# An adaLN block on one core: the second gate moved from w2 to the finished tiles, its weights loaded late, and a new instruction order

## The chip, the cores and the metric

The kernel runs on one core of a Trainium2 chip. A core has five engines, each with its own instruction queue that is worked off in order: TensorE (PE, matrix products; PEld is its weight load), VectorE (DVE), ScalarE (ACT), GpSimd (POOL) and SyncE (SP, which here issues nearly all DMA transfers). They are held together by semaphores alone: an instruction that waits holds up everything behind it in its queue. The metric is the device time of one execution in microseconds (us); the profile's span runs from the first to the last instruction.

## The reference

x has 2048 rows of 512 numbers in bf16. A condition c gives six vectors: two shifts, two scales, two gates.

```python
mod = (_silu(c) @ w_mod).reshape(c.shape[0], 6, 1, -1)
sa, ca, ga, sb, cb, gb = (mod[:, 0].copy(), mod[:, 1].copy(), mod[:, 2].copy(), mod[:, 3].copy(), mod[:, 4].copy(), mod[:, 5].copy())
h = _layernorm(x, axis=-1) * (1 + ca) + sa
x = x + ga * _A_ref(h, A_wqkv, A_wo)
h = _layernorm(x, axis=-1) * (1 + cb) + sb
x = x + gb * _B_ref(h, B_w1, B_w3, B_w2)
```

`_A_ref` is attention with 32 heads of 16, in which a row looks at eight rows: itself and those 2, 4, ... 14 rows before it. `_B_ref` is `(silu(h @ w1) * (h @ w3)) @ w2` with 1792 hidden columns. gb is the second gate: it multiplies the columns of the feed-forward output before it is added to x.

## The kernel before

The rows are cut into 16 tiles T of 128. Everything stays in on-chip memory but v, which goes through a scratch tensor in DRAM so that the shifted rows can be gathered by DMA.

The program is written as a list of operations (`p.op`, `p.dma`, line 82 on), each with its engine and the values that it reads and writes. It is not emitted in the order of the text: the table `ORDER` (line 980) is a permutation of all operations, and each engine gets its own operations in that order. `SLOTS` (line 1028) says which buffer of its pool (PSUM bank, q, v, vsh, output buffer and so on) each value gets. Waits follow from both: for the values read, and for the earlier users of a buffer. The numbers beside each operation (its cost) are only notes for whoever made the order; they change nothing in the instructions.

The stages, as the text has them:

- **Constants and loads.** SP issues x, w_mod in pieces (`wm_s` for shifts and scales, `wm_g` for the gates; `wm_g[i]` lie in a region that the feed-forward stage later takes for its hidden tiles), wqkv, wo, w1, w3, w2 in four parts each.
- **Modulation.** Per output column a few matmuls with one moving column. `gate(i)` (line 522) makes gate i: 16 small matmuls from `wm_g[i]`, `gcol` copied by DVE (537), four matmuls that spread it over all partitions (541), and an ACT copy to `ga_bc` or `gb_bc` (547). ga is multiplied into wo (946), gb into w2 in four parts (952, values `w2_scaled`), both on DVE.
- **First layer norm, q, k, v** over the groups `LN1`: tiles 0-1, 2-3, then fours. `ln_stats` (549) takes mean and variance on DVE (555, 556), adds epsilon (DVE for tiles 0 and 1, POOL otherwise), raises to -1/2 on POOL (565), and normalizes on DVE (576; tile 0 has a form of its own, 571). It runs over pairs of tiles, for tiles 0 and 1 over each tile alone. `ln_T` (609) transposes on PE (636) or by DMA (617) and applies scale and shift, on ACT (644, 621) or, for the first half of the first group, on DVE (651). For the first group the projections run piece by piece, one input quarter at a time (`pieces`, 611, and `proj`, 665).
- **Attention**, in blocks of two tiles (the last of four): products of q with shifted k on DVE (742), sums over a head on PE (752), maximum, subtraction, sum, reciprocal and weights on DVE (764 to 797), exponential on ACT (782), a turn of the weights on PE (807) and its copy by ACT (811), products with the gathered v on DVE (827), sums on PE (855), a copy by ACT (861), a DMA transpose, the output projection (867) and the residual on DVE (871), which also sums x for the next norm.
- **Second layer norm** (`ln_sums`, 582): minus the mean on POOL (586), squares on ACT (590), then three steps on POOL (596 variance, 597 power, 599 bias), the normalized tiles on ACT (601); transposes and shift/scale as above.
- **Feed-forward** over the groups `FFN`: tiles 0-1, 2-3, 4-7, 8-11, 12-13, 14-15. Per group and hidden block fi of 128 columns (14 blocks): four matmuls with w1 (883), silu on ACT (889), four with w3, the product on DVE (892). Then per tile `ffn_w2` (899): 14 matmuls of 512 columns in two halves into one PSUM bank (921), for tiles 14 and 15 in two column halves (909), and `store`: DVE adds x (931) and SP stores.

PE, DVE and ACT work at several stages at once: the feed-forward of early groups stands between the attention of later tiles.

## Time and profile before

| | |
|---|---|
| times of three runs | 239.48, 238.94, 238.96 us (median 238.96) |
| profiled execution | span 237.7 us; 1.26 below the median of the runs |
| granted TensorE clock | 1.000 |
| loads through the main DMA queue | 38.56 MB |
| DMA transposes of normalized tiles, issue to landing | 3.7 us (median of 20) |
| loads of 512 KB parts of w1, w3, w2, issue to landing | 7.9 us (median of 6) |

In the views, a row of the timeline gives start and length in us, engine, line, operation, output and inputs by the program's names, how many instructions were merged, and in brackets the idle time before it with what ended it. `pall` is PSUM. A row of a group gives busy time, mean duration in ns, and idle time before. In the table by stage the columns are the stretch, its length, and the busy time (and number of instructions) of PE, PEld, DVE, ACT and POOL, then the clock, the DMA share and GB/s. Matmuls are pipelined: one of 512 columns shows as 379 ns, while a new one starts every 216.

### The profile page before, as it was taken

To read this page: it belongs to the slowest core of one execution; us is meant where nothing else is said; L and a number is where in the kernel's file an instruction comes from. 1 tells how busy PE (TensorE), PEld (TensorE's weight loads), DVE (VectorE), ACT (ScalarE), POOL (GpSimd) and SP (SyncE) were. 2 spreads that over 40 slices of the span, in tenths; PEclk is the share of its full clock that TensorE was granted. 3 is DMA by queue.
4 is the path that set the end of the run, shared out by engine and by line. 5 is a ranking of instruction groups with operands and counts; after the bars stand their busy time and mean duration, and the time that the engine had idled before them with its cause. 6 is when DMAs were issued, how large, how long until landed. Compare 5 with 4: busy or idle time off the path is not lost.

```text
span 237.7 us, 4535 instructions
## 1 busy us (share of the span) xinstructions
PE 229.7 (97%) x1781; PEld 136.2 (57%) x1806; DVE 179.4 (75%) x279; ACT 138.5 (58%) x267; POOL 29.2 (12%) x66
## 2 busy tenths in 40 slices
PE   7999999999999998999999999999999999999995
PEld 4776454445588674664444444444475457485774
DVE  5699999999999989999999999682654403434433
ACT  2289577999978744985865594837473405040300
POOL 4434100013002000240002520012010000000000
PEclk9999999999999999999999999999999999999999
DMA  6999999999999999897981693642203000000202
GB/s 216 372 337 322 158 237 299 208 269 283 353 200 270 243 249 199 173 260 177 247 234 47 182 234 72 154 132 46 67 19 91 3 0 0 6 19 0 70 0 88
DMA packets 46317, 38.85 MB, mean 163 GB/s; under 512 B 21704, under 2 KB 37080, under 8 KB 46296
## 3 DMA queue, kind: packets, MB, share of 16 engines
q1 hardware_dynamic: 46288, 38.56, 66.9%
q8 instruction: 14, 0.23, 0.4%
q14 instruction: 7, 0.06, 0.1%
q10 hardware_dynamic: 8, 0.00, 0.0%
HBM read 29.62 MB, written 4.21 MB: 142 GB/s over the span
## 4 chain that ended last, share of the span: by engine, by line
PE 74%; DMA 8%; DVE 8%; SPq 4%; ACT 3%; issue 2%; ACTq 0%; DVEq 0%
PE pall L883 38%; PE pall L921 18%; DMA sb_x<-in_A_x_dram 5%; PE pall L867 5%; SPq L124 4%; PE pall L691 4%; DMA sb_vsh<-v_scratch_dram 3%; PE pall L909 3%; PE pall L855 2%; PE pall L752 2%; PE pall L711 2%; DVE sb_vsh L827 2%; DVE sb_pq L742 2%; DVE sb_hh L892 1%; ACT sb_h L621 1%
## 5 line engine op out<-in xcount | busy, mean ns | idle before, releaser
L883 PE MATMUL pall<-sb_h,sb_w 128*128 128x256 bf16 (+1 forms) x664 | 101.9, 307 | 1.8 <-DVE sb_hh L892 0.9
L883 PEld LDWEIGHTS pall<-sb_h,sb_w 128*128 128x128 bf16 x672 | 64.8, 98 | 37.2 <-issue 2.8
L889 ACT ACTIVATE sb_sg<-pall 128x256 bf16<-128x256 f32 (+1 forms) x84 | 35.6, 453 | 54.1 <-PE pall L883 53.0
L892 DVE TENSOR_TENSOR sb_hh<-sb_sg,pall 128x256 bf16<-128x256 bf16 (+1 forms) x84 | 39.9, 505 | 34.8 <-PE pall L883 32.7
L921 PE MATMUL pall<-sb_w,sb_hh 128*128 128x512 bf16 x190 | 44.0, 379 | 0.3
L742 DVE TENSOR_TENSOR sb_pq<-sb_q,sb_kT 128x4096 bf16<-128x4096 bf16 x16 | 36.3, 2282 | 0.0
L921 PEld LDWEIGHTS pall<-sb_w,sb_hh 128*128 128x128 bf16 x196 | 19.0, 98 | 21.6 <-DVE sb_hh L892 0.4
L691 PE MATMUL pall<-sb_h,sb_wqkv 128*128 128x512 bf16 (+1 forms) x154 | 30.2, 335 | 0.5 <-issue 0.2
L827 DVE TENSOR_TENSOR sb_vsh<-sb_vsh,sb_al 128x4096 bf16<-128x4096 bf16 x12 | 27.3, 2287 | 2.1 <-DMA sb_vsh<-v_scratch_dram 2.1
L621 ACT ACTIVATE sb_h<-sb_h,sb_modc 128x512 bf16<-128x512 bf16 (+1 forms) x24 | 16.5, 743 | 10.1 <-DMA sb_h<-sb_xn 10.1
L691 PEld LDWEIGHTS pall<-sb_h,sb_wqkv 128*128 128x128 bf16 x160 | 14.7, 98 | 11.8 <-ACT sb_ac L861 0.4
L931 DVE TENSOR_TENSOR sb_o<-pall,sb_x 128x512 bf16<-128x512 f32 (+1 forms) x18 | 11.1, 625 | 10.5 <-PE pall L921 6.8
L711 PE MATMUL pall<-sb_wqkv,sb_h 128*128 128x512 bf16 x62 | 15.5, 379 | 0.2
L867 PE MATMUL pall<-sb_wo,sb_ot 128*128 128x512 bf16 x61 | 15.3, 379 | 0.3 <-issue 0.2
L586 POOL TENSOR_SCALAR sb_nm<-sb_sx 128x2 f32<-128x2 f32 x8 | 1.7, 218 | 105.2 <-DVE sb_x L871 105.1
L644 ACT ACTIVATE sb_h<-pall,sb_modc 128x256 bf16<-128x256 bf16 (+1 forms) x18 | 9.9, 612 | 7.5 <-DVE sb_modc L509 6.5
L861 ACT ACTIVATE sb_ac<-pall 128x512 bf16<-128x512 f32 x16 | 9.5, 595 | 7.2 <-PE pall L855 7.1
L601 ACT ACTIVATE sb_xn<-sb_x,sb_nb,sb_rs 128x512 bf16<-128x512 bf16 x16 | 12.4, 806 | 0.7 <-POOL sb_nb L599 0.6
L871 DVE SCALAR_TENSOR_TENSOR sb_x<-pall,sb_x 128x512 bf16<-128x512 f32 x16 | 10.9, 686 | 1.5 <-PE pall L867 1.3
L590 ACT ACTIVATE sb_xn<-sb_x,sb_nm 128x512 bf16<-128x512 bf16 x16 | 11.4, 714 | 0.7 <-POOL sb_nm L586 0.7
L721 ACT ACTIVATE sb_v<-pall 128x512 bf16<-128x512 f32 x16 | 9.5, 600 | 2.8 <-PE pall L711 2.8
L555 DVE BATCH_NORM_STATS2 sb_st<-sb_x 128x6 f32<-128x512 bf16 x16 | 10.6, 680 | 0.8 <-DMA sb_x<-in_A_x_dram 0.7
(87 smaller groups left out, 208.3 us busy)
## 6 DMA issues: line engine op xcount, KB each, us to landing
sb_vsh<-v_scratch_dram SPq DMA_DIRECT2D x48, 256.0 KB, 5.5
sb_vshx<-v_scratch_dram SPq DMA_DIRECT2D x16, 256.0 KB, 4.6
sb_w<-in_B_w_dram SPq DMA_DIRECT2D x6, 512.0 KB, 7.9
sb_w<-in_B_w_dram SPq DMA_DIRECT2D x6, 384.0 KB, 5.4
v_scratch_dram<-sb_v SPq DMA_DIRECT2D x16, 128.0 KB, 6.4
out_dram<-sb_o SPq DMA_DIRECT2D x14, 128.0 KB, 1.8
sb_wqkv<-in_A_wqkv_dram SPq DMA_DIRECT2D x6, 256.0 KB, 6.3
sb_x<-in_A_x_dram SPq DMA_DIRECT2D x4, 256.0 KB, 6.4
```

Of the source, the lines that this page charges most:

```text
L590: p.op("act", lambda e, vn=vn, T=T: e.activation(vn.at[:], x_sb[:, T, :], ACT.Square, bias=nm[:, T, :], accum_out=var[:, T, :]), c_act(512 ...
L601: p.op("act", lambda e, vn=vn, T=T: e.activation(vn.at[:], x_sb[:, T, :], ACT.Identity, bias=nb[:, T, :], scale=rs[:, NT + T, :]), c_act(5 ...
L621: return e.activation(vh.at[:, ft, 0:n * P], vh.at[:, ft, 0:n * P], ACT.Identity, bias=modc[:, 8 * which + ft:8 * which + ft + 1], scale=m ...
L691: ins = e.matmul(bank(vp)[:, j * n:(j + 1) * n], wqkv[:, t, col:col + P], vh.at[:, t, 0:n], start=(t == ORDER[0] and j == 0), stop=(t == O ...
L711: ins = e.matmul(bank(vp), vh.at[:, t, tt * P:(tt + 1) * P], wqkv[:, t, 2 * D:3 * D], start=(t == ORDER[0]), stop=(t == ORDER[-1]))
L742: return e.tensor_tensor(vp.at[:], in0, in1, ALU.mult)
L827: return e.tensor_tensor(v_w, v_w, a_w, ALU.mult)
L867: ins = e.matmul(bank(vy), vt.at[:, ft, :], wo[:, ft, :], start=(ft == 0), stop=(ft == KT - 1))
L883: ins = e.matmul(bank(vp)[:, 0:n], wt[:, t, fi * P:(fi + 1) * P], vh.at[:, t, 0:n], start=(t == 0), stop=(t == KT - 1))
L889: p.op("act", lambda e: e.activation(vt.at[:, 0:n], bank(vgp)[:, 0:n], ACT.Silu), c_act(n), k, r=[vgp], w=[vt], table="silu")
L892: p.op("dve", lambda e: e.tensor_tensor(vh_.at[:, 0:n], vt.at[:, 0:n], bank(vup)[:, 0:n], ALU.mult), c_dve(n), k, r=[vt, vup], w=[vh_])
L921: ins = e.matmul(bank(vz), vhh[fi].at[:, tt * P:(tt + 1) * P], w2[:, fi, :], start=(fi == 0), stop=(fi == NF - 1))
```

## The change

- **w2 is not scaled in place.** The four DVE multiplications are gone, and tiles 0 to 11 use w2 as loaded. Their finished PSUM tile is copied by ACT to the output buffer, multiplied there by `gb_bc` on DVE, and x is added by a second DVE operation.
- **Tiles 12 to 15** still use a scaled w2, but a copy: two DVE operations (blocks 0 to 7, 8 to 13) write it to buffers of the vsh pool, once the attention tiles that used those are done. These tiles are stored as before.
- **The second gate's weights** get no place of their own: they are loaded into q buffer 0, and in the new order `gate(1)` runs after the output projections of tiles 7 and 6 instead of within the first projections.
- **Tiles 0 and 1** take their statistics as a pair: one epsilon and one power for both, and tile 0 is normalized like all others. The second group too is projected piece by piece, with the first half of its shift/scale on DVE.
- **`ORDER` and `SLOTS` are new as a whole.** On SP the two first parts of w2 now come behind the gathers for tiles 5 and 4 (before, ahead of them), the gate's weights behind the last part of w2. On PE, behind the output projection of tile 1, the new order has four key/query groups, the turn for tiles 2 and 3 and the values of tiles 12 and 14 before the transposes of the first feed-forward pair (before: seven key/query groups, the turn, and the values of tiles 13 and 14). On DVE, behind the residuals of tiles 0 and 1, it has sum, reciprocal and weights of tiles 2 and 3 and then the query product of tile 5, the value product of tile 3, the query product of tile 7 (before: sum, reciprocal and weights, the sum for tiles 4 and 5, a small copy, the query product of tile 7). On ACT the copy of those weights stands between the two normalized tiles 1 and 0. The first scaled copy of w2 stands behind the value product of tile 12 and ahead of the residuals of tiles 13 and 12.

```diff
-    wm_g = [at([P, KT, 512], bf, f"wm_g{i}", 12288 * i + 8192) for i in range(2)]
+    wm_g0 = at([P, KT, 512], bf, "wm_g0", 8192)
...
-    vwms, vwmg = [Val("wms0"), Val("wms1")], [Val("wmg0"), Val("wmg1")]
+    vwms, vwmg = [Val("wms0"), Val("wms1")], [Val("wmg0"), Val("wmg1", qpool)]
...
-    late["wmg1"] = p.dma(wm_g[1][:], wm_view[:, :, 2560:3072], ("load", 13), (512, 1024), w=[vwmg[1]])
+    late["wmg1"] = p.dma(lambda: vwmg[1].at[:], wm_view[:, :, 2560:3072], ("load", 13), (512, 1024), w=[vwmg[1]])
...
-            if T == 0:
-                p.op("dve", lambda e, vn=vn, T=T: e.scalar_tensor_tensor(vn.at[:], x_sb[:, T, :], mv[:, T, 0:1], bass.AP(rs, T, [[2 * NT, P], [0, D]]),
-                                                                         op0=ALU.subtract, op1=ALU.mult), 600, ("nm", T),
-                     r=[vx[T], vr] + vms, w=[vn])
-                vns.append(vn)
-                continue
...
-        vh.pieces = [Val(f"h_{ft}") for ft in range(KT)] if not which and not gi else None
+        vh.pieces = [Val(f"h_{ft}") for ft in range(KT)] if not which and gi < 2 else None
...
-                if not half and not which and gi < 1:
+                if not half and not which and gi < 2:
...
-    vw2s = [Val(f"w2_scaled{g}") for g in range(NG)]
+    w2v = [Val(f"w2_scaled{i}", vshpool) for i in range(2)]
...
+        def scaled(fi, c0, n):
+            return w2v[fi // 8].at[:, fi % 8, c0:c0 + n]
...
-                    ins = e.matmul(bank(vz), vhh[fi].at[:, tt * P:(tt + 1) * P], w2[:, fi, :], start=(fi == 0),
-                                   stop=(fi == NF - 1))
+                    ins = e.matmul(bank(vz), vhh[fi].at[:, tt * P:(tt + 1) * P], scaled(fi, 0, D) if T >= NT - 4 else w2[:, fi, :],
+                                   start=(fi == 0), stop=(fi == NF - 1))
...
-        store(T, 0, D, vz)
+        if T >= NT - 4:
+            store(T, 0, D, vz)
+            return
+        vo = Val("o", opool)
+        k = ("zo", T)
+        p.op("act", lambda e: e.activation(vo.at[:], bank(vz), ACT.Copy), c_act(512), k, r=[vz], w=[vo])
+        o = p.op("dve", lambda e: e.tensor_tensor(vo.at[:], vo.at[:], gb_bc[:], ALU.mult), 340, k, r=[vg[1]], w=[vo], lock=True)
+        p.op("dve", lambda e: e.tensor_tensor(vo.at[:], vo.at[:], x_sb[:, T, :], ALU.add), 340, k, r=[vx[T]], w=[vo], lead=o, lock=True)
+        finals.append(p.dma(out2d[T * P:(T + 1) * P, :], lambda: vo.at[:], k, (128, 1024), r=[vo], cost=400, store=True))
...
-        vns = [v for pr in ([[T] for T in Ts] if gi == 0 else pairs(Ts)) for v in ln_stats(pr)]
+        vns = [v for pr in pairs(Ts) for v in ln_stats(pr)]
...
-    for g in range(NG):
-        a, b = cuts[g], cuts[g + 1]
-        p.op("dve", lambda e, a=a, b=b: e.tensor_tensor(w2[:, a:b, :], w2[:, a:b, :],
-                                                      bass.AP(gb_bc, 0, [[D, P], [0, b - a], [1, D]]), ALU.mult),
-             48 + 274 * (b - a), ("mod", 7 + g), r=[vw2[g], vg[1]], w=[vw2s[g]], lock=True)
...
+        if Ts[-1] == NT - 3:
+            for i, (a, b) in enumerate(((0, 8), (8, NF))):
+                p.op("dve", lambda e, i=i, a=a, b=b: e.tensor_tensor(w2v[i].at[:, 0:b - a, :], w2[:, a:b, :],
+                                                                     bass.AP(gb_bc, 0, [[D, P], [0, b - a], [1, D]]), ALU.mult),
+                     48 + 274 * (b - a), ("mod", 7 + i), r=vw2 + [vg[1]], w=[w2v[i]], lock=True)
...
 ORDER = [
-    8, 9, 10, 0, 20, 21, 22, 3, 4, 1, 2, 16, 17, 23, 24, 25, 26, 27, 28, 29, 30, 31, 32, 34, 33, 18, 59, 60, 61, 62, 63, 64, 11,
...
+    8, 9, 10, 0, 20, 21, 22, 3, 4, 1, 2, 16, 17, 23, 24, 25, 26, 27, 28, 29, 30, 31, 32, 34, 33, 18, 59, 60, 61, 62, 63, 64,
```

12 lines of the change are left out of this document (6 added, 6 removed), and 132 rows, old and new, of tables (ORDER, SLOTS).

## The prediction

> **What bounds the kernel now.** I read first the page's busy times and its 40 slices.
>
> ```profile
> span 237.7 us, 4535 instructions
> PE 229.7 (97%) x1781; PEld 136.2 (57%) x1806; DVE 179.4 (75%) x279; ACT 138.5 (58%) x267; POOL 29.2 (12%) x66
> PE   7999999999999998999999999999999999999995
> DVE  5699999999999989999999999682654403434433
> ```
>
> PE is busy nearly everywhere, DVE only up to slice 25 (150 us). A PE that is "busy" may still wait inside, so the second step was to ask at what rate it works: the chain that ended last holds 28 matmuls of 512 columns in 6.04 us, 0.216 each, and the same rate stands wherever the chain runs through PE alone.
>
> ```profile
> 137.05 6.04 PE pall L883 x28
> 143.10 0.22 PE pall L807 x4
> 228.91 6.13 PE pall L909 x56
> ```
>
> A group of four 512-column matmuls thus costs 0.86 us, one of four 256-column matmuls 0.44 (56 in 6.13), a turn of the attention weights 0.22. The third view is the busy time of each engine by stage, from the first projection (8.2) to the last matmul (235.1):
>
> ```profile
> 8.20:20.00 11.80, 11.54 (x113) 8.68 (x116) 9.95 (x31) 8.88 (x17) 3.87 (x10) 1.00 1.10 332
> 20.00:60.00 40.00, 39.51 (x344) 20.13 (x351) 39.70 (x48) 33.56 (x64) 5.44 (x9) 1.00 1.16 254
> 60.00:98.00 38.00, 36.38 (x355) 25.04 (x351) 36.03 (x53) 27.72 (x57) 1.53 (x5) 1.00 1.07 237
> 98.00:150.00 52.00, 51.31 (x380) 26.06 (x385) 51.57 (x63) 34.77 (x63) 9.94 (x15) 1.00 0.75 186
> 150.00:190.00 40.00, 39.68 (x221) 20.32 (x223) 20.91 (x34) 22.39 (x45) 3.98 (x8) 1.00 0.28 71
> 190.00:235.10 45.10, 44.87 (x321) 31.41 (x321) 15.82 (x35) 9.58 (x25) 0.00 (x0) 1.00 0.07 23
> ```
>
> The columns after the length are PE, PEld, DVE, ACT, POOL. PE's idle time by stage is 0.26, 0.49, 1.62, 0.69, 0.32 and 0.23, in all 3.61 us of 226.9. The change neither adds nor removes a matmul of any weight (the 32 small gate matmuls move only), and head and tail keep their form; so **the time changes by what these 3.61 us become**. The fourth view, the waits, says what makes the 1.62:
>
> ```profile
> PE pall L883 <- DVE sb_hh L892: 0.9, 1, 0.9
> PE pall L855 <- DVE sb_vsh L827: 0.4, 1, 0.4
> ```
>
> PE stands there because DVE is late. Where DVE has room (150 to 190) PE still idles 0.32 in 40 us, 0.008 per us: that is the floor. Above it lie 1.62 - 0.30 = 1.3 us in 60 to 98, and 0.69 - 0.42 = 0.3 in 98 to 150. More than 1.6 us can't be won from DVE's relief.
>
> **The parts.** *Scaling of w2 taken off DVE's full stage.*
>
> ```profile
> L952 DVE TENSOR_TENSOR sb_w<-sb_w,sb_gb_bc x4: 952/1084/1218, 68.0 to 95.0; 128x2048 bf16<-128x2048 bf16 x2, 128x1536 bf16<-128x1536 bf16 x2
> 89.82 1.05 PE L883 MATMUL pall<-sb_h,sb_w 128*128 128x256 bf16 x8 [0.87 <-DVE sb_hh L892]
> L651 DVE TENSOR_SCALAR sb_h<-pall,sb_modc 128x256 bf16<-128x256 bf16 x2 | 0.7, 404 | 0.2 <-PE pall L636 0.2
> ```
>
> 4.3 us (two of 1.22, two of 0.95) leave DVE between 68 and 96 us, the two large ones ahead of PE's 0.87 us wait at 89. The first tile's own form of normalization gives way to the common one, and two evacuations of the second pair (0.4 each) come from ACT to DVE. Gain on PE: at best the 1.6 us above, at worst nothing. I take 1.4, since the lost time sits where the relief falls.
>
> *What comes back late.* The two sizes differ by 0.266 us for 512 columns, so the scaled copies of 8 and 6 tiles cost 0.15 + 8 x 0.266 = 2.28 and 1.75 on DVE, behind the value products of tiles 12 and 13 and inside the last-but-one feed-forward group. On each of 12 finished tiles the one DVE addition from PSUM becomes an ACT copy and two DVE operations of 0.15 + 0.27 = 0.42 (extrapolated).
>
> ```profile
> L931 DVE TENSOR_TENSOR sb_o<-pall,sb_x 128x512 bf16<-128x512 f32 x14 | 9.5, 682 | 6.8 <-PE pall L921 6.8
> L861 ACT ACTIVATE sb_ac<-pall 128x512 bf16<-128x512 f32 x16 | 9.5, 595 | 7.2 <-PE pall L855 7.1
> ```
>
> That is 0.84 for 0.68 on DVE, 1.9 us in all, and 12 x 0.6 = 7.1 us on ACT. It lies in stages where DVE is idle 19 of 40 and 29 of 45 us and ACT 18 and 35; only four copies come earlier, where ACT is idle 17 of 52. I take 0. Without that cover the copy behind tile 12's product holds up DVE by 2.28, so 0 to +1.5 on PE (the first group behind tile 12's reduction, 0.86, needs nothing from DVE).
>
> *Loads.* The gate's second weights (512 KB) leave the crowded start and are issued behind w2's last quarter. The q buffer that they take was last read 60 us earlier.
>
> ```profile
> sb_wm_g<-in_w_mod_dram SPq DMA_DIRECT2D x2, 512.0 KB, 10.0
> 87.70 1.11 SPq L124 DMA_DIRECT2D sb_w<-in_B_w_dram  x2
> 92.09 3.57 SPq L124 DMA_TRANSPOSE sb_ot<-sb_ac  x2
> ```
>
> Its gate matmuls stand on PE directly behind tile 6's output projection. The loads ahead of it on SP wait for the value reduction of tile 4. From there to the gate PE has four half output tiles of seven 512-column matmuls (6.0 us), four projections (3.5), ten groups of 256 columns (4.4) and four tiled reductions, about 16 us; SP has an evacuation to wait for (0.6 and a signal), two transposes (1.8 each) and five loads (0.55 each) to issue, 6.4, and then 10.0 to landing: 17.3. At worst 1.3 us, with a quieter queue nothing; I take 0. Between the new issue of w2's first half and its first use PE has by the same count some 15 us: 0.
>
> *Joint statistics of tiles 0 and 1, and the second pair in pieces.* The first pair's matmuls start when DVE's first evacuation ends, and that waits for the second tile's transposes:
>
> ```profile
> 6.93 0.41 DVE L576 TENSOR_SCALAR sb_xn<-sb_x,sb_mv,sb_rs 128x512 bf16<-128x512 bf16 x1 [0.46 <-POOL sb_rs L565]
> 7.72 0.73 DVE L651 TENSOR_SCALAR sb_h<-pall,sb_modc 128x256 bf16<-128x256 bf16 x2 [0.21 <-PE pall L636]
> 11.02 0.74 DVE L576 TENSOR_SCALAR sb_xn<-sb_x,sb_mv,sb_rs 128x512 bf16<-128x512 bf16 x2 [1.05 <-POOL sb_rs L565]
> ```
>
> With one power on POOL for both, the second tile's normalization ends near 7.0 instead of 7.34, but the small modulation matmuls stand between the two tiles' transposes as before, so the evacuation comes at the same 7.7. Afterwards the last shift/scale column comes before the second pair's statistics, which end some 0.3 later; their normalized tiles are ready at 11.8 and 12.2 instead of from 11.4 on, and PE has only the first pair's 32 matmuls of 256 columns (3.5 us from 8.2, so to 11.7) ahead of their transposes. It waits some 0.4, and its old idle time here was 0.26: +0.2, between -0.3 and +0.6.
>
> **The new order's tight place.** The first feed-forward pair's normalization runs through POOL. Before, it went like this:
>
> ```profile
> 47.83 1.90 PE L867 MATMUL pall<-sb_wo,sb_ot 128*128 128x512 bf16 x8
> 50.72 0.09 DVE L871 DVE_READ_ACCUMULATOR sb_x<-pall,sb_x 128x1 f32 x1
> 50.90 0.22 POOL L586 TENSOR_SCALAR sb_nm<-sb_sx 128x2 f32<-128x2 f32 x1 [20.98 <-DVE sb_x L871]
> 52.03 0.69 DVE L797 TENSOR_TENSOR sb_attn<-pall,sb_ssum 128x512 bf16<-128x512 f32 x1
> 52.64 0.68 DVE L794 TENSOR_REDUCE sb_ssum<-pall 128x64 f32<-128x512 f32 x1
> 52.75 0.19 POOL L596 TENSOR_SCALAR sb_rs<-sb_var 128x2 f32<-128x2 f32 x1 [1.64 <-ACT sb_xn L590]
> 53.03 0.71 POOL L597 TENSOR_TENSOR sb_rs<-sb_rs,sb_cst 128x2 f32<-128x2 f32 x1
> 53.31 2.28 DVE L742 TENSOR_TENSOR sb_pq<-sb_q,sb_kT 128x4096 bf16<-128x4096 bf16 x1
> 53.81 1.82 POOL L599 TENSOR_TENSOR sb_nb<-sb_nm,sb_rs 128x2 f32<-128x2 f32 x1
> 55.67 1.52 ACT L601 ACTIVATE sb_xn<-sb_x,sb_nb,sb_rs 128x512 bf16<-128x512 bf16 x2
> 57.56 0.61 PE L636 MATMUL pall<-sb_ident,sb_xn 128*128 128x128 bf16 x8
> ```
>
> POOL's last step took 1.82 us, not 0.20: it began inside DVE's 2.28 us product and ended 0.04 after it. The same shows elsewhere (the first one free, the second begun inside the product of 158.73 to 161.02):
>
> ```profile
> 140.68 0.19 POOL L596 TENSOR_SCALAR sb_rs<-sb_var 128x2 f32<-128x2 f32 x1 [1.70 <-ACT sb_xn L590]
> 158.73 2.29 DVE L827 TENSOR_TENSOR sb_vsh<-sb_vsh,sb_al 128x4096 bf16<-128x4096 bf16 x1 [0.85 <-DMA sb_vsh<-v_scratch_dram]
> 159.52 1.55 POOL L596 TENSOR_SCALAR sb_rs<-sb_var 128x2 f32<-128x2 f32 x1 [1.94 <-ACT sb_xn L590]
> ```
>
> Before, PE had nine groups of four and a turn between tile 1's output projection (ends 49.57) and these transposes, 8.0 us, and did not wait. In the new order it has six and a turn: 6 x 0.86 + 0.22 = 5.4 us. And on DVE tile 5's query product follows directly on the weights of tiles 2 and 3 (before, two shorter steps came between). Count from the end of tile 1's residual (50.81 above = 0): DVE's next operation after the weights starts at 52.64 = 1.83; POOL's variance step at 52.75 = 1.94. It comes 0.11 after the product has begun, so it ends with it, at 1.83 + 2.28 + 0.04 = 4.15; the power (0.09 + 0.71) and the bias (0.07 + 0.20) end at 5.2, ACT's first normalized tile (0.04 + 0.81) at 6.1. The residual itself ends about 1.5 after that projection: the logit reduction stands 4 groups (3.45) ahead of the projection's end, and behind it DVE has maximum and subtraction (0.61 each from start to start, as between 52.03 and 52.64), a product (2.28) and two residuals (0.6 and 0.8), with 0.1 of delay: 5.0. So the transposes, due 5.4 after the projection, can start at 7.6: **PE waits 2.2 us**. ACT makes the second tile only after the copy of the weights (0.6), 0.3 later than PE's one group in between: +0.3. DVE, whose next value product waits for that same copy, idles 2.6, which uses up the early relief; but PE is late by as much, so I leave the 1.4 standing. Bounds for the place: 1.1 (POOL's steps partly through) to 2.6.
>
> A rule of the Trainium skill bears on this: "SBUF — State Buffer", section "Who interferes with whom", says that an operation of DVE with two SBUF inputs and one of GpSimd that reads SBUF exclude each other for the whole instruction, and that the one that starts first wins. The trace has it one way only: the product began at 53.31 while the power step ran until 53.74, and took its usual 2.28. By the rule a POOL step that slips in first would delay DVE by its 0.2 to 0.7 and PE by nothing more, and the sum would be lower by up to 0.2; I go by the rows.
>
> **Sum** against the profiled span: -1.4 (DVE's relief) + 2.5 (first pair) + 0.2 (head) + 0 + 0 = +1.3, a span of 239.0. The median is 238.96, 1.26 above the span; with that kept, **240.3 us**. The bounds of the terms give -1.6 + 1.1 - 0.3 = -0.8 and 0 + 2.6 + 0.6 + 1.5 + 1.3 = +6.0; all at one end at once is unlikely, and its own range is 239.2 to 241.5.
>
> **Rivals.** *Relief without the wait (faster):* DVE reaches tile 5's product 1.4 us later than I count, for instance because the exponentials before it are late on a full ACT (33.56 of 40), so POOL's three steps pass in 1.3 us. Then -1.6 + 0.2 = -1.4: 237.6. For it: DVE is relieved exactly where PE waited. Against: the same late ACT also delays the squares that POOL waits for. *A draw:* PE comes to the transposes late for another reason and waits 1.1 instead of 2.5: 238.96 - 1.4 + 1.1 + 0.2 = 238.9. *DVE's late stage:* the first scaled copy stands between tile 12's value product and two residuals on which the next normalization hangs. If DVE is as late there as it was before (51.57 of 52 us busy up to 150), those 2.28 us come out on PE, less 0.8 of covered matmuls, on top of the forecast: 241.8. Against: PE has 5.8 us of matmuls before the second of those residuals. *The gate's weights land late* at tile 6: +1.3, 241.6; it decides only if landing takes the full 10.0 us, a figure from the crowded first 30 us.
>
> **Chances.** Forecast 0.44; faster rival 0.28; draw 0.13; late DVE stage 0.10; late gate weights 0.05. About 0.3% (0.7 us) is what a measurement of this kernel can tell from none. Faster 0.29 (its rival and a little of the draw), within 0.3% 0.15, slower 0.56. As cases of both signs hold most of the chance, the range reaches from the faster rival less some spread, 237.0, to the late rivals' 241.9.
>
> **What would show it.** In the stage table PE's idle time: about 2.5 us new in a wait of PE's transposes (L636) for ACT's normalized tile at about 54 to 57 us, POOL's variance step (L596) there near 2 us long and ending with a product, DVE idle 2 to 3 us behind tile 5's product, and PE's wait for the hidden products at 89 us gone. If the transposes of the first pair don't wait, I am wrong by the sign. If waits stand behind 150 us or at the gate's matmuls, the late rivals hold.

## The result, and the profile after

The changed kernel takes 244.89 us (median of 4 runs, 244.11 to 245.47) against 239.11 (238.94 to 239.48): a ratio of 1.0246, 95% interval 1.0217 to 1.0276, so 5.8 us slower. The prediction said 240.3, with a range that ended at 241.9. A run with a granted clock of 0.99 instead of 1.00 takes about 2 us longer, and as most runs of before beside f1, f2, f3 and f5 below were such (240.4 to 242.5 us, the others 238.3 to 239.5), the ratios of these four read low: at 1.00 on both sides they are 1.021, 1.019, 1.021 and 1.001.

The profiled execution has a span of 243.0 us; before it was 237.7. The first view is again the busy time by stage (PE, PEld, DVE, ACT, POOL behind the length), now of the changed kernel.

```profile
8.20:20.00 11.80, 11.77 (x104) 8.60 (x102) 10.20 (x30) 7.85 (x15) 4.53 (x10) 1.00 1.10 329
20.00:60.00 40.00, 37.48 (x321) 17.36 (x319) 35.52 (x46) 30.79 (x58) 6.07 (x10) 1.00 1.05 240
60.00:98.00 38.00, 37.24 (x369) 26.01 (x368) 35.05 (x45) 27.11 (x60) 1.31 (x4) 1.00 0.90 234
98.00:150.00 52.00, 49.58 (x377) 24.68 (x376) 49.59 (x72) 34.90 (x63) 5.32 (x16) 1.00 0.83 184
150.00:190.00 40.00, 40.00 (x233) 19.95 (x232) 24.66 (x35) 21.28 (x41) 1.31 (x4) 1.00 0.30 78
190.00:240.40 50.40, 50.40 (x349) 33.81 (x347) 20.72 (x47) 17.21 (x40) 1.31 (x4) 1.00 0.09 26
```

PE's idle time is now 0.03, 2.52, 0.76, 2.42, 0.00 and 0.00 us. Nothing is lost behind 150 us, where the rival of the late DVE stage looked for it. Nor is anything lost at the gate's matmuls, where the rival of the late gate weights looked; PE's row there has no wait:

```profile
105.62 0.54 PE L531 MATMUL pall<-sb_csT_bf,sb_q 128*128 128x1 bf16 x16
```

What is seen of the loss stands in five waits, which PE's timeline of the same kernel names (start, length, line, the waited time and its releaser in brackets):

```profile
47.77 2.17 PE L861 MATMUL pall<-sb_wo,sb_ot 128*128 128x512 bf16 x8 [0.95 <-DMA sb_ot<-sb_ac]
56.80 0.40 PE L630 MATMUL pall<-sb_ident,sb_xn 128*128 128x128 bf16 x4 [1.46 <-ACT sb_xn L595]
96.55 0.61 PE L849 MATMUL pall<-sb_vsh,sb_ind 128*32 128x512 bf16 x8 [0.76 <-DVE sb_vsh L821]
100.42 3.20 PE L918 MATMUL pall<-sb_w,sb_hh 128*128 128x512 bf16 x14 [1.43 <-DMA sb_w<-in_B_w_dram]
118.37 1.04 PE L877 MATMUL pall<-sb_h,sb_w 128*128 128x512 bf16 x4 [0.99 <-ACT sb_h L615]
```

In order these are: the output projections of tiles 0 and 1 for their transposes; the first feed-forward pair's transposes for the normalized tile (the predicted place); tile 6's value reduction, for a DVE product that itself stood 1.00 for tile 6's value load; the second half of the w2 product of tiles 1 and 0 for the last quarter of w2; the first feed-forward group of tiles 4 to 7 for its shifted and scaled input. They show 5.6 us. Of the waits of before, 0.23 at 63.9 us and the 0.87 and 0.36 at 89.8 and 93.2, none is left, so the waits in the rows grew by 4.1 us of the 5.8; which rows hold the rest isn't known. And a wait that is shown isn't yet a price: the experiments had to tell which of them, once taken away, stays away.

The predicted place came out as worked out, operation by operation (DVE, POOL, ACT, DVE of the changed kernel):

```profile
52.51 2.28 DVE L736 TENSOR_TENSOR sb_pq<-sb_q,sb_kT 128x4096 bf16<-128x4096 bf16 x1
52.62 2.22 POOL L590 TENSOR_SCALAR sb_rs<-sb_var 128x2 f32<-128x2 f32 x1 [1.63 <-ACT sb_xn L584]
55.93 0.81 ACT L595 ACTIVATE sb_xn<-sb_x,sb_nb,sb_rs 128x512 bf16<-128x512 bf16 x1 [1.80 <-POOL sb_nb L593]
57.26 2.29 DVE L821 TENSOR_TENSOR sb_vsh<-sb_vsh,sb_al 128x4096 bf16<-128x4096 bf16 x1 [2.48 <-ACT sb_al L805]
```

The end of the residual is 50.67 here; the product starts 1.84 after it (predicted 1.83) and POOL's variance step 1.95 after it (1.94), takes 2.22 us instead of about 0.2 and ends with the product. DVE then idles 2.48 (predicted 2.6).

### The profile page after: what moved, and what is told of

Read it like the earlier page. It is cut to its first block, busy times and chain, and to the rows that moved or that the text cites. A ratio compares the mean times of both kernels' runs of the same rounds, so it can differ in the third digit from the quotient of the medians.

```text
span 243.0 us, 4568 instructions
## 1 busy us (share of the span) xinstructions
PE 232.6 (96%) x1806; PEld 134.7 (55%) x1806; DVE 180.8 (74%) x290; ACT 140.7 (58%) x275; POOL 22.6 (9%) x65
## 4 chain that ended last, share of the span: by engine, by line
PE 80%; ACT 7%; DMA 5%; SPq 2%; POOL 2%; DVE 1%; issue 1%; ACTq 0%
PE pall L877 38%; PE pall L918 14%; PE pall L685 9%; PE pall L861 4%; PE pall L705 4%; PE pall L906 3%; PE pall L849 2%; DMA sb_w<-in_B_w_dram 2%; SPq L124 2%; PE pall L746 2%; ACT sb_xn L584 2%; PE pall L630 1%; DMA sb_ot<-sb_ac 1%; ACT sb_xn L595 1%; ACT sb_h L615 1%; POOL sb_rs L590 1%
## 5 line engine op out<-in xcount | busy, mean ns | idle before, releaser
L918 PE MATMUL pall<-sb_w,sb_hh 128*128 128x512 bf16 x168 | 37.6, 379 | 1.4 <-DMA sb_w<-in_B_w_dram 1.4
L821 DVE TENSOR_TENSOR sb_vsh<-sb_vsh,sb_al 128x4096 bf16<-128x4096 bf16 x13 | 29.5, 2284 | 3.5 <-ACT sb_al L805 2.5
L685 PE MATMUL pall<-sb_h,sb_wqkv 128*128 128x512 bf16 (+1 forms) x160 | 31.6, 337 | 0.0
L918 PEld LDWEIGHTS pall<-sb_w,sb_hh 128*128 128x128 bf16 x168 | 16.3, 98 | 21.3 <-DMA sb_w<-in_B_w_dram 1.9
L861 PE MATMUL pall<-sb_wo,sb_ot 128*128 128x512 bf16 x64 | 15.8, 380 | 1.1 <-DMA sb_ot<-sb_ac 1.0
L705 PE MATMUL pall<-sb_wqkv,sb_h 128*128 128x512 bf16 x64 | 16.4, 379 | 0.0
L929 ACT ACTIVATE sb_o<-pall 128x512 bf16<-128x512 f32 x12 | 7.0, 591 | 11.2 <-PE pall L918 11.2
L638 ACT ACTIVATE sb_h<-pall,sb_modc 128x256 bf16<-128x256 bf16 (+1 forms) x16 | 8.7, 622 | 5.9 <-DVE sb_modc L509 5.5
L861 PEld LDWEIGHTS pall<-sb_wo,sb_ot 128*128 128x128 bf16 x64 | 5.9, 98 | 8.6 <-issue 1.6
```

Source lines behind the costliest of these rows:

```text
L685: ins = e.matmul(bank(vp)[:, j * n:(j + 1) * n], wqkv[:, t, col:col + P], vh.at[:, t, 0:n], start=(t == ORDER[0] and j == 0), stop=(t == O ...
L705: ins = e.matmul(bank(vp), vh.at[:, t, tt * P:(tt + 1) * P], wqkv[:, t, 2 * D:3 * D], start=(t == ORDER[0]), stop=(t == ORDER[-1]))
L821: return e.tensor_tensor(v_w, v_w, a_w, ALU.mult)
L861: ins = e.matmul(bank(vy), vt.at[:, ft, :], wo[:, ft, :], start=(ft == 0), stop=(ft == KT - 1))
L918: ins = e.matmul(bank(vz), vhh[fi].at[:, tt * P:(tt + 1) * P], scaled(fi, 0, D) if T >= NT - 4 else w2[:, fi, :], start=(fi == 0), stop=(f ...
```

## The experiments

Each kernel ran beside the kernel before on the same chip. The median of before was 239.3 to 240.8 beside these runs, so the ratios to it are what is compared; for the changed kernel it is 1.0246.

| kernel | us | ratio to before, 95% | what it is |
|---|---|---|---|
| e1_w2_loads_early | 247.46 | 1.0309 (1.0267 to 1.0352) | changed; w2's second half loaded at 82 us |
| e2_product_behind_value | 242.71 | 1.0147 (1.0117 to 1.0177) | changed; the swap on DVE |
| e3_transposes_first | 244.70 | 1.0214 (1.0179 to 1.0249) | changed; two transposes ahead of a load |
| p1_new_parts_old_order | 249.81 | 1.0452 (1.0406 to 1.0498) | before; new arithmetic of w2 |
| e4_w2_loads_in_gap | 243.86 | 1.0152 (1.0099 to 1.0204) | changed; w2's second half loaded at 54 us |
| e5_gap_and_swap | 243.60 | 1.0148 (1.0099 to 1.0198) | e4 and swap |
| e6_gap_swap_transposes | 245.37 | 1.0209 (1.0150 to 1.0267) | e5, transposes first, evacuations first |
| p1b_new_parts_stores_late | 243.66 | 1.0145 (1.0090 to 1.0201) | p1, four stores and a copy later |
| p1c_gate_by_dve_from_psum | 240.51 | 1.0072 (1.0038 to 1.0106) | p1 without work on ACT |
| p2_copies_only | 241.92 | 1.0100 (1.0054 to 1.0147) | before; copies of finished tiles on ACT, stores as in p1b |
| e7_loads_in_gap | 245.57 | 1.0213 (1.0148 to 1.0277) | swap; four loads of w1 and w3 at 54 us, w2's second half at 65 us |
| e9_copy_behind_norm | 249.79 | 1.0439 (1.0389 to 1.0488) | swap; copy of tile 1 later |
| f1_squares_first | 243.99 | 1.0145 (1.0097 to 1.0194) | swap; two squares earlier |
| f2_w2_two_places | 243.72 | 1.0134 (1.0087 to 1.0182) | swap; last quarter of w2 2.5 us earlier |
| f3_both | 245.26 | 1.0153 (1.0090 to 1.0217) | f1 and f2 |
| f5_before_product_ahead | 239.65 | 0.9993 (0.9948 to 1.0038) | before; one hidden product earlier |
| h1_w2_half_back | 246.53 | 1.0261 (1.0222 to 1.0300) | changed; w2's first half at its old place |
| h2_w2_half_back_swap | 244.92 | 1.0200 (1.0160 to 1.0241) | h1 and swap |

### The swap: the predicted place, undone

```
 DVE  ... attention weights 2,3
-     tile 5 query product   tile 3 value product   tile 7 query product
+     tile 3 value product   tile 5 query product   tile 7 query product
 PE   tile 5's logit reduction behind the third feed-forward group
```

> The changed kernel with one edit in DVE's order: tile 5's query product goes behind tile 3's value product instead of ahead of it, and on PE tile 5's logit reduction three groups later, behind the third feed-forward group. Theory of separate waits: POOL's variance step for tiles 0 and 1 then meets no DVE product and takes about 0.2 us instead of 2.2; the transposes of that pair start at about 55.1 instead of 56.8 us, and 1.6 us less is left at the end: 243.3 against 244.9. Rival, DVE is the bound: DVE idles through the same time for the copy of the attention weights and is 0.5 us later afterwards, so PE meets it at the next products and keeps at most 0.5: 244.4 or more.

It came to 242.71: of the ratio 0.0099 went, 2.4 us (2.2 in the medians). POOL's step and PE's waits after the swap:

```profile
52.69 0.19 POOL L590 TENSOR_SCALAR sb_rs<-sb_var 128x2 f32<-128x2 f32 x1 [1.63 <-ACT sb_xn L584]
66.76 0.62 PE L746 MATMUL pall<-sb_pq,sb_E 128*32 128x256 bf16 x16 [1.00 <-DVE sb_pq L736]
98.90 3.19 PE L918 MATMUL pall<-sb_w,sb_hh 128*128 128x512 bf16 x14 [0.73 <-DMA sb_w<-in_B_w_dram]
116.31 1.04 PE L877 MATMUL pall<-sb_h,sb_w 128*128 128x512 bf16 x4 [0.45 <-ACT sb_h L615]
```

2.22 us became 0.19, PE no longer waits for the pair's transposes, and the gain stays to the end, though DVE, now later, makes PE wait 1.00 at 66.76. That the product held up POOL's step, and PE with it, is settled. The gain, however, is only in part the predicted one. At the place itself 1.46 goes and 1.00 comes back: the feed-forward matmuls behind it start at 67.32 instead of 67.82, 0.5 earlier. The rest seems to come by way of the loads. SP stands at the store of tile 9's values until ACT has copied them, and that copy is queued behind the two normalized tiles (SP in the changed kernel, then after the swap):

```profile
61.24 0.33 SPq L124 DMA_DIRECT2D v_scratch_dram<-sb_v  x1
```
```profile
59.47 0.33 SPq L124 DMA_DIRECT2D v_scratch_dram<-sb_v  x1
```

With this store 1.8 us earlier, the last quarter of w2 is issued at 93.37 instead of 94.85, and PE goes on with it at 98.90 instead of 100.42, 1.5 earlier. This second part rests on one trace of each kernel: in f1, which has the same order on SP and this store at 59.87, the quarter was issued at 95.20 and PE waited 1.43 for it again.

### The relief of DVE, by itself

To see what the new arithmetic is worth without the new order, it was put into the kernel before:

```
-    for g in range(NG):          # four scalings of w2, 4.3 us of DVE
-        p.op("dve", ... tensor_tensor(w2[:, a:b, :], w2[:, a:b, :], gb_bc ...
+    tiles 0 to 11, in place of the one addition:
+    p.op("act", ... activation(vo, bank(vz), ACT.Copy))          # p1, p1b
+    p.op("dve", ... tensor_tensor(vo, vo, gb_bc, mult))
+    p.op("dve", ... tensor_tensor(vo, vo, x, add))
+    p1c: no ACT copy, tensor_tensor(vo, bank(vz), gb_bc, mult) on DVE
+    two scaled copies of w2 for tiles 12 to 15, late on DVE
```

> The kernel before, in its own order of work, with only the arithmetic of w2 changed: the four scalings of w2 leave DVE, w2 is used as loaded, the finished tiles 0 to 11 are copied by ACT and multiplied and added by DVE, and two scaled copies for tiles 12 to 15 are made late on DVE (at about 172 and 177 us). The gate's weights, the first pair's normalization and the order of everything else stay. Theory: the parts cost nothing, the loss is made by the new order's waits; relief of DVE by 4.3 us between 68 and 96 us gives 0 to 1.6 us, so 237.4 to 239.0. Rival: the late work is what costs (twelve copies on ACT, twelve more operations and 4 us of scaled copies on DVE), so 240.5 or more even in the old order.

> As the earlier run of the new arithmetic of w2 in the order of before, which stood 3.9 us behind a value load that SP had queued behind a store, and 2.9 us of DVE behind a copy of a finished tile on ACT. Now those four stores follow the last value loads, and that copy follows the weights' copy. Theory: these two queue places were all of its loss of 10 us beyond about 3 (the wait of 3.9 with a clock dip behind it); 241 to 243 remains, from the finished tiles' copies that hold up ACT ahead of the squares and evacuations of tiles 4 to 7 (1.1 us of PE's wait at 115). Rival: the new work itself is at fault wherever it stands, 246 or more. Rival: it only needed free queues, 239.5 or less.

> The kernel before in its own order with w2 unscaled, as in the earlier two runs of that kind, but with no work added on ACT: each finished tile of 0 to 11 is multiplied by the gate straight from PSUM on DVE (0.68) and then added (0.42), at the place where its one addition stood, and its store keeps its place. DVE loses 4.3 us between 68 and 96 and gains twelve times 0.42 and the two late scaled copies. Theory: of the 3 to 4 us that the old order lost with the copies on ACT, the copies are the cause, because ACT waits for a finished tile with the squares of tiles 4 to 7 behind it; without them the old order is at 237.8 to 239.5, up to 1 us faster than before. Rival: the multiplications and scaled copies on DVE are the cause; 241 or more.

p1 was spoilt by its own making: a store, placed ahead of tile 14's value loads on SP's queue, waited for a finished tile, and PE stood 3.85 us for that tile's reduction. With four stores and one copy later (p1b) 243.66 was left, a little above what was expected. p1c, with nothing added on ACT, is at 240.51: nearer to before, but slower, and not faster as the theory had it. A part of its loss is in a new wait, for a value product on DVE (it starts at 126.44, in before at 125.39), behind the extra operations of 0.42 us for two finished tiles:

```profile
129.38 0.61 PE L855 MATMUL pall<-sb_vshx,sb_ind 128*32 128x512 bf16 x8 [0.73 <-DVE sb_hh L892]
```

So the time of p1c alone doesn't tell what the relief is worth. But the wait that the relief was to remove is still there, in the stage and the place where the prediction had seen it (p1c: the stage row, then DVE, then PE):

```profile
60.00:98.00 38.00, 36.58 (x358) 25.17 (x358) 32.83 (x49) 27.57 (x56) 1.52 (x5) 1.00 1.06 232
87.30 2.29 DVE L827 TENSOR_TENSOR sb_vsh<-sb_vsh,sb_al 128x4096 bf16<-128x4096 bf16 x1 [1.05 <-DMA sb_vsh<-v_scratch_dram]
89.98 1.05 PE L883 MATMUL pall<-sb_h,sb_w 128*128 128x256 bf16 x8 [0.88 <-DVE sb_hh L892]
```

DVE is busy 32.83 us of the stage instead of 36.03, and PE's wait at 89 us for a hidden product is 0.88 instead of 0.87. The row of DVE says why, and the kernel before has the same one:

```profile
87.14 2.29 DVE L827 TENSOR_TENSOR sb_vsh<-sb_vsh,sb_al 128x4096 bf16<-128x4096 bf16 x1 [1.04 <-DMA sb_vsh<-v_scratch_dram]
```

DVE wasn't late because of its amount of work. It stood 1.04 us for tile 7's value load, with four hidden products queued behind that value product. Five kernels in the old order bear it out: PE's wait follows DVE's wait for the transfer, not the scaling. In p2 the wait is gone with all the scaling still on DVE:

| kernel | scaling of w2 on DVE | DVE's wait for the load | PE's wait at 89 |
|---|---|---|---|
| before | yes | 1.04 | 0.87 |
| p1c | no | 1.05 | 0.88 |
| p1 | no | 0.40 | 0.22 |
| p2 | yes | 0.27 | none |
| p1b | no | none | none |

The last run took one hidden product out from behind the load, in the kernel before:

```
 DVE  ... maximum 8,9
+     hidden product 3 of the second pair
      tile 7 value product
-     hidden product 3 of the second pair
      three more hidden products
```

> The kernel before with one edit on DVE: the first of the four hidden products behind tile 7's value product goes ahead of it, into the 1.0 us in which DVE stands for that product's value load (its inputs are ready at 86.8, the load at 87.1). Theory, the queue: PE's wait of 0.9 for a hidden product at 89.8 us shrinks to at most 0.45, and the kernel gains 0.4 to 0.9: 238.1 to 238.7 against 239.1. Rival, DVE's load: the value product comes as much later as the hidden product takes, PE waits for tile 7's reduction instead, and nothing changes: within 0.3 of before.

```profile
91.11 0.61 PE L883 MATMUL pall<-sb_h,sb_w 128*128 128x256 bf16 x4 [0.48 <-DVE sb_hh L892]
```

The wait is 0.48 instead of 0.87, as the queue has it, but the time didn't move beyond what can be told (0.9948 to 1.0038). No version faster than the kernel before came out of these runs.

### The copies of the finished tiles

p2 has the copies, with w2 scaled as before; four stores and the copy of tile 7 stand where p1b has them:

```
-    p.op("dve", ... tensor_tensor(vo, bank(vz), x, add))
+    p.op("act", ... activation(vo, bank(vz), ACT.Copy))
+    p.op("dve", ... tensor_tensor(vo, vo, x, add))
```

> The kernel before, with its scaling of w2, and one thing alone added: the finished tiles 0 to 11 are first copied from PSUM by ACT, and DVE adds from that copy (the stores and the copy of tile 7 placed as in the second run with copies). Theory of the copies on ACT: 241.5 to 243, with the squares of tiles 4 to 7 held up behind the first copy and PE waiting 1 to 1.5 us at about 115 us for the evacuation of these tiles. Rival: a copy costs nothing; 238.5 to 239.7.

241.92, 1.0% or 2.4 us more than before, within the theory's numbers. ACT of p2 (first two rows), then PE:

```profile
97.00 0.60 ACT L932 ACTIVATE sb_o<-pall 128x512 bf16<-128x512 f32 x1 [1.72 <-PE pall L921]
97.62 1.28 ACT L889 ACT_TABLE_LOAD   x1
99.35 1.49 PE L883 MATMUL pall<-sb_h,sb_w 128*128 128x256 bf16 x12 [1.08 <-ACT sb_sg L889]
114.70 6.29 PE L883 MATMUL pall<-sb_h,sb_w 128*128 128x512 bf16 x28 [1.11 <-ACT sb_h L621]
```

A copy costs ACT 0.6, which its idle time would hide. What isn't hidden is that ACT stands 1.72 us for PE to finish the tile, with a table load, an activation and the squares of tiles 4 to 7 queued behind the copy: PE waits 1.08 for the activation at once, and 1.11 for the evacuation of tiles 4 to 7 fifteen us later. Before, neither wait was there, and p1c, without copies, has neither.

The changed kernel has the same stand, longer (ACT):

```profile
102.15 0.60 ACT L929 ACTIVATE sb_o<-pall 128x512 bf16<-128x512 f32 x1 [4.02 <-PE pall L918]
```

Two runs tried to take it away there, both with the swap:

```
 ACT (e9)                               ACT (f1)
-copy of finished tile 1                -copy of finished tile 1
 squares of tiles 4, 5                   squares of tiles 4, 5
 ... normalization of tile 7            +copy of finished tile 1
+copy of finished tile 1
```

> The changed kernel with tile 5's query product behind tile 3's value product (242.7 alone), and on ACT the copy of the finished tile 1 behind the normalization of tile 7 instead of ahead of the squares of tiles 4 and 5. In the changed kernel ACT stood 4.0 us at that copy, until PE had finished the tile, while the squares' input was there 1.9 us earlier. Theory of ACT's order: the normalized tiles 4 and 5 come 1.9 us earlier, the four transposes no longer crowd, and PE's wait of 0.5 for the evacuation of tiles 4 to 7 goes: 242.2 or less. Rival: tiles 6 and 7 set that evacuation, and their chain starts from their residuals, which come when they came: no gain, 242.5 or more.

> The changed kernel with tile 5's query product behind tile 3's value product (242.7 alone), and on ACT the squares of tiles 4 and 5 ahead of the copy of the finished tile 1 instead of behind it. ACT stood 4 us at that copy while the squares' input was there 1.4 us or more before PE finished the tile. Theory, ACT's order is a cause: the chain of tiles 4 and 5 comes 1 to 1.8 us earlier, the transposes of the four tiles end earlier, and the 0.5 us of PE's wait at 116 go: 242.2 or less. Rival, tiles 6 and 7 set it: 242.5 to 242.9.

e9 was wrong in both its cases, by 7 us. PE's row:

```profile
110.95 1.04 PE L877 MATMUL pall<-sb_h,sb_w 128*128 128x256 bf16 x4 [5.28 <-ACT sb_o L929]
```

The copy also frees the finished tile's PSUM bank, and PE waits for that bank. Early, the copy holds up ACT; late, it holds up PE. In f1 the squares went first and the wait at 118 was 0.52, as after the swap alone (0.45); the time is no better either. So in the new order the squares of tiles 4 and 5 aren't what that wait hangs on. That leaves tiles 6 and 7, as the rival had it; no run moved those.

### The loads

Where PE waited at 100 us for the last quarter of w2, eight runs moved loads. The theory was that the wait could be removed; the rival, that the queue passes it on.

```
 SP   order in the changed kernel, with start times:
      w1.1 (53.7) | standing 7 us | store 9 (61.2), w3.1, store 7, transpose 3, w3.3, w1.2, transpose 2, w3.2,
      values 5, store 12, values 4, w2.0 w2.1 (76.3), values 7 (78.7), values 6 (86.9),
      transpose 4, w2.2 (91.7), transpose 5, values 8 (two of four), w2.3 (94.9), gate weights
e1    w2.2 and w2.3 behind values 7
e4    w2.2 and w2.3 behind w1.1
e5    e4 and the swap
e7    w3.1, w3.3, w1.2, w3.2 behind w1.1, w2.2 and w2.3 behind transpose 3; and the swap
f2    w2.3 directly behind w2.2; and the swap      (f3: and f1)
h1    w2.1 behind w3.1, w2.0 behind store 7, as before   (h2: and the swap)
```

> The changed kernel with one edit on the queue of SP: the loads of the third and fourth quarter of w2 are issued right behind the value loads of tile 7 (about 81 us) instead of between the transposes of tiles 4 and 5 and behind the first value loads of tile 8 (91.7 and 94.9 us). Theory of separate waits: PE's rows show four places where it falls behind, and the largest, the second half of the w2 product of tiles 1 and 0 at 100.4 us, waits for that last quarter; the wait of 1.4 us shown there and what hides in the busy matmuls around it come to 2.5 us, and nothing takes it back, so 242.4 against 244.9. Rival, DVE is the bound: between 98 and 150 us DVE has 2.4 us of idle time and all of it lies in waits for PE, so that an earlier PE meets a late DVE product; then at most 1.0 us is kept, 243.9 or more.

> The changed kernel with one edit on SP's queue: the loads of w2's third and fourth quarter are issued at about 54.3 us, behind the second quarter of w1, where SP's queue stands idle for 7 us and the transfers run at 0.6 to 0.8 of the time, instead of at 91.7 and 94.9. The run before, which put them at 82 us, showed the wait for w2 gone and a wait of 2.5 us for tile 6's value product in its place: there they pushed tile 6's value loads back. Theory of separate waits: at 54 us nothing needed soon stands behind them, so both waits are absent, 2.5 us are gained, 242.4 against 244.9. Rival, the transfer rate is the bound through all of 20 to 100 us: what goes first only moves the wait to the next load (the later quarters of w1 and w3 at 66 us, or the value loads of tiles 5 and 4), and at most 0.8 is gained, 244.1 or more.

> Both edits together: tile 5's query product behind tile 3's value product (alone 242.7) and the two loads of w2 in the gap of SP's queue. Theory of separate waits: the gains add, 2.2 of the swap and 2.5, or the 0.7 of wait for w2 that the swap had left plus what hides around it (1.2 to 1.9): 240.2 to 241.5. Rival, another resource takes over: no better than the swap alone, 242.3 or more.

> The changed kernel with tile 5's query product behind tile 3's value product (242.7 alone), and on SP the four later loads of w1 and w3 issued in the gap at 54 us, ahead of the stores of tiles 9 and 7, with w2's third and fourth quarter in the places that become free behind tile 3's transpose (about 62 us). Theory of queue places: SP's 7 us of standing behind a store are used, the wait for w1/w3 at 67 us and for w2 at 99 us are both gone, and 0.7 to 1.5 less than the swap alone remains: 241.2 to 242.0. Rival, the transfers are bound by their rate: the waits move to the values' stores and loads, and nothing is gained: 242.4 or more.

> The changed kernel with tile 5's query product behind tile 3's value product (242.7 alone), and the load of w2's last quarter directly behind that of its third, ahead of tile 5's transpose and of two value loads of tile 8, so 2.5 us earlier and behind all value loads of tile 6. Theory, a place in the queue: PE's wait of 0.7 for it at 99 us and what hides around it go, and nothing needed sooner is pushed back by more than 0.6: 241.5 to 242.0. Rival, the transfer rate: tile 5's projection or tile 8's values wait in its place; 242.5 or more.

> The three edits together. Theory: the gains add, 241.0 to 241.7. Rival, the wait at 116 takes back what is won at 99, since the chain behind tile 6's residual has a fixed length of 12 to 13 us against 11.9 us of PE's work: no better than the better of the two alone.

> The changed kernel with the part of the change that loads the first half of w2 later undone: its two loads go back to where they stood in SP's order before, around the store of tile 7's values at 61 us instead of behind tile 4's value loads at 76. Theory, the megabyte moved out of 60 to 70 us is what makes w2's last quarter late: the value loads of tiles 7 and 6 and all of w2's second half come earlier, PE's wait at 100 us goes, and 1.5 to 2.5 us with it: 242.4 to 243.4 against 244.9. Rival, the queue passes its lateness on wherever a load is put, as in the runs with w2's second half moved: 244.2 or more, with a new wait for a quarter of w1 or w3 at 66 or for values between 66 and 97.

> That edit and tile 5's query product behind tile 3's value product. Theory: the two gains add, 240.2 to 241.3, within 1% of the kernel before. Rival: no better than the swap alone, 242.3 or more.

Of these only e4 is clearly faster than the kernel it was made from, by about as much as the swap (0.0094 of the ratio, with intervals that nearly touch), and together they bring no more than one of them (e5). Most lost the wait they aimed at and had another; h1 and h2 kept 0.59 and 1.18 of it. The new wait, from PE's timelines of e1, e4, e5, e7, f2 and h1:

```profile
99.22 1.04 PE L849 MATMUL pall<-sb_vsh,sb_ind 128*32 128x512 bf16 x8 [2.53 <-DVE sb_vsh L821]
```
```profile
67.37 0.61 PE L877 MATMUL pall<-sb_h,sb_w 128*128 128x256 bf16 x4 [0.76 <-DMA sb_w<-in_B_w_dram]
```
```profile
67.03 0.61 PE L877 MATMUL pall<-sb_h,sb_w 128*128 128x256 bf16 x4 [1.94 <-DMA sb_w<-in_B_w_dram]
```
```profile
68.95 0.62 PE L849 MATMUL pall<-sb_vsh,sb_ind 128*32 128x512 bf16 x8 [2.98 <-ACT sb_v L715]
```
```profile
98.20 1.67 PE L861 MATMUL pall<-sb_wo,sb_ot 128*128 128x512 bf16 x7 [1.41 <-DMA sb_ot<-sb_ac]
```
```profile
72.30 2.54 PE L877 MATMUL pall<-sb_h,sb_w 128*128 128x256 bf16 x12 [1.99 <-DMA sb_w<-in_B_w_dram]
```

That is: tile 6's values, a quarter of w1 or w3 (twice), the copy of values whose buffer waits for a store, a transpose, and again a quarter of w1 or w3. In e1 DVE says it directly: its product for tile 6 stood for the value load.

```profile
96.87 2.29 DVE L821 TENSOR_TENSOR sb_vsh<-sb_vsh,sb_al 128x4096 bf16<-128x4096 bf16 x1 [2.85 <-DMA sb_vsh<-v_scratch_dram]
```

h1 was made from two rows of each kernel, before and then changed (the last columns are the DMA share and GB/s):

```profile
60.00:70.00 10.00, 9.77 (x116) 7.42 (x110) 9.66 (x13) 8.29 (x18) 0.00 (x0) 1.00 1.26 291
90.00:101.00 11.00, 10.59 (x78) 6.09 (x79) 10.86 (x22) 8.45 (x17) 1.49 (x5) 1.00 0.82 189
```
```profile
60.00:70.00 10.00, 10.00 (x106) 6.22 (x105) 8.99 (x8) 9.34 (x19) 0.00 (x0) 1.00 0.70 188
90.00:101.00 11.00, 8.81 (x84) 5.42 (x82) 10.00 (x13) 3.34 (x9) 0.22 (x1) 1.00 1.00 263
```

Between 60 and 70 us the new order moves 103 GB/s less, which is a megabyte in 10 us, just the first half of w2; between 90 and 101 it moves more. It looked like the cause. Put back to its old place, the half won nothing: h1 is at 1.0261, no better than the changed kernel, and h2, at 1.0200, no better than the swap alone. The theory that the moved half alone is the cause is refuted. In h2 PE still waited 1.18 for the last quarter of w2, whose own place in the queue, behind two value loads of tile 8, hadn't moved.

### The first output projections

```
 SP (e3)  store 6
-         w1.3   transpose 0   store 10   transpose 1
+         transpose 0   store 10   transpose 1   w1.3
 (e6: with e5, and on ACT the evacuations of tiles 12 to 15 ahead of the copy of tile 7's values)
```

> The changed kernel with one edit on the queue of SP: the transposes of the attention outputs of tiles 0 and 1 are issued ahead of the last quarter of w1, with only the store of tile 10's values between them (before the edit: w1's quarter, transpose 0, store, transpose 1). Theory of separate waits: the output projections of tiles 0 and 1 start about 1.5 us earlier than at 47.8 us, the residuals and all that hangs on them move by as much, and the end with them: 243.4 against 244.9. Rival: the chain through the residual, the logits and POOL's blocked variance step is set by DVE's order and not by the projections, so the transposes of the first feed-forward pair still start near 56.8 us and the end moves by less than 0.4: 244.5 or more.

> The kernel of the two edits, and the transposes of the attention outputs of tiles 0 and 1 ahead of w1's last quarter on SP, and on ACT the four shift-and-scale evacuations of tiles 12 to 15 ahead of the copy of tile 7's values. The transposes alone gave nothing, because PE then waited 1.4 us for those evacuations. Theory of two things being late at one place (projections' transposes and the evacuations behind them): 1.0 to 1.4 less than the kernel of the two edits. Rival: tile 1's residual still meets DVE's fixed order, so less than 0.4.

244.70 and 245.37: nothing won that can be told. In e3 the projections started at 46.51 instead of 47.77, and then PE waited 1.41 us for the shifted input of tiles 12 to 15, whose evacuation ACT reaches at the old time; the transposes of the first pair still waited 1.58. In e6 that wait was gone, and five others of 0.5 to 0.8 stood between 57 and 69 us. The wait for the transposes is real in the profile, but taking it away won nothing: a second thing is late at the same place.

## Why the prediction was wrong

Its sum was -1.4 + 2.5 + 0.2 + 0 + 0 = +1.3; the result is +5.8.

- **"I take 1.4, since the lost time sits where the relief falls."** This step failed. That a stage is full for DVE and that PE waits there for DVE doesn't make DVE's amount of work the cause: the row ahead of the late products, a wait of 1.04 for a value load, had it, and the prediction didn't quote DVE's row there. In p1c PE's wait stayed at 0.88 with 3.2 us less work on DVE. In the changed kernel it is gone, as the prediction's signs had it, but p2 shows that it goes without relief when the load is there in time; and the waits of 60 to 98 us fell only from 1.46 to 0.76, since a new one for tile 6's values came. The floor of 0.008 per us, and the 0.3 us above it in 98 to 150, were weak as well: the trace of before has 1781 matmul records where PE's weight loads number 1806, so 25 are missing, and a missing record looks like idle time. Four groups there that are one matmul short show 0.16 each ahead of them, with nothing that released them.
- **"That is 0.84 for 0.68 on DVE ... I take 0"** for the twelve copies on ACT. This step failed too. It set the copies against ACT's idle time and didn't ask what is queued behind a copy that waits for PE. In the old order the copies cost 1.0% (0.5 to 1.5), 2.4 us (p2). Their price in the new order couldn't be taken out by itself: e9 shows that the copy can't go as late as behind tile 7's normalization, f1 that the squares behind it aren't the limit. The part of the same step on the scaled copies held: PE doesn't idle between 150 and 190.
- **"Loads ... 0."** The gate's weights were in time, as said: the gate's matmuls don't wait. For w2 the count covered its first half only; the last quarter, issued at 94.9 behind value loads, made PE wait 1.43. Taken away by itself (e4) this was worth about 2 us, but nothing beside the swap (e5), where PE waited 1.94 for a load of w1 or w3 instead.
- **The tight place** was right in place, in mechanism and in the offsets counted from the residual. The term was +2.5; PE's wait shows 1.46. The step that was off: the residual ended 0.9 us after the projection (49.77 to 50.67), not 1.5, because the projection had itself started 0.95 late, and DVE stood 0.18 and 0.44 for it ahead of the two residuals. Undoing the place won 2.2 to 2.4, near the 2.5, but that is partly luck: by the traces about 0.5 was won there, and the rest later, with loads that came earlier, which the prediction didn't count. The Trainium skill ("SBUF — State Buffer", section "Who interferes with whom") has the rule by which the two exclude each other; the 0.19 of the same step without a product beside it agrees.
- **The head** was put at +0.2; PE's idle time up to 20 us went from 0.26 to 0.03. A small error of sign; 0.16 of the 0.26 was a wait for a part of wqkv.
- **No term at all** stood for the waits at 47.8, 96.6 and 118. Taking away the first won nothing (e3). The second is for tile 6's value load. The third has a counterpart in p2, with the copies as its cause; in the changed kernel its price stays open.

The rivals: the relief without the wait fell with the wait; the draw was right that the wait would be shorter (1.46) for another reason, the late projections, but it needed the relief. The late DVE stage fell, since PE is never idle behind 150 us, and the late gate weights fell at 105.62, where the gate's matmuls start without a wait. The bounds of the terms did reach +6.0, but they were set aside as unlikely to come together, and the term that was furthest off, the copies, had bounds that only its scaled half was worth.

How the 5.8 us are made up is settled in part. The swap accounts for 2.2 to 2.4. What is left after it, 1.0147, is as much as the new arithmetic of w2 costs in the old order (p1b, 1.0145), but the waits lie elsewhere, so this agreement of sizes is no proof. Why the loads of the new order come late between 45 and 100 us, when the same loads in the old order do not, stays open in the main. One part is seen: behind the load at 53.73 SP stands 6.9 us at the store of tile 9's values (5.0 after the swap), where before the longest of its stands between 53 and 64 us was 2.8; no run moved that store, and e4, the one move of loads that won, put loads ahead of it (so did e7, which won nothing). Every order of SP's queue that was tried left PE waits between 57 and 102 us, and the difference that the rates point to, w2's first half, isn't the cause by itself.

## What to carry to other kernels

When an engine is called late, read the row ahead of its late instruction: a busy engine may still stand there for a transfer, and work taken off it then doesn't bring that instruction forward. Price an instruction added to an in-order engine by what is queued behind it and what it waits for, and not by its length against the engine's idle time; a copy out of PSUM has a deadline on both sides. In a transfer queue that is worked off in order, moving one load mostly moves the wait: count what the load is put ahead of, and look for the store that the queue stands at.
